# Attention, then routed experts on one core: another order of work where the two meet

## The chip, the cores and the metric

The kernel runs on one core of a Trainium2 chip. The metric is device microseconds (us) of one execution; the kernel before has a median of 485.14 us over three runs (483.79 to 489.23). TensorE does the matmuls, VectorE, ScalarE and GpSimd the elementwise work, and SP issues most of the transfers. In the profile they are PE (PEld for its weight loads), DVE, ACT, POOL and SP.

## The reference

Attention with sinks and a window, then a two-level choice of one expert out of 16 for each of the 3072 tokens:

```
q, k, v: 4 batches x 8 heads x 768 positions x 64
scores = q k^T / 8, kept where key is a sink (first 4) or 0 <= row - key < 128
a = softmax(scores);  attn = a v;  x = attn as 3072 tokens x 512
group = argmax(x w_group) of 4;  expert = argmax(x w_expert[group]) of 4
y = max(x w1[expert], 0) w2[expert]          w1: 512 x 1024, w2: 1024 x 512
out = softmax weight of the group * softmax weight of the expert * y
```

## The kernel before

Everything is one function, moe_attention, whose instructions are written in the order in which each engine is to run them (the class Pinned keeps it so). All its instructions are recorded at line 104, the wrapper; they are told apart by the tiles that they write and read.

**Attention** is a software pipeline over 24 tiles of 128 positions, with all eight heads of a tile together. The loop `for i in range(NI + 2)` works in step i on tile i (scores, maxima, exponentials), on tile a = i - 1 (transposes, values) and on tile b = i - 2 (normalising, routing logits). The helpers of a step are: `scores` (PE, tile ps), `maxima` (DVE, tile sm), `exps` (ACT, tile pt), `trans` (PE transposes of pt into tp), `evac` (ACT copy tp to pw), `halves` (POOL product of pw with a triangle), `sink_copy` (POOL), `sink_t` and `sink_evac` (PE and ACT, tile spT), `values` (PE, 32 small products pw with vv into po), `sink_values` (PE, 8 products into po), `out_evac` (ACT copy of po to xT), `natural` (PE transposes of xT into another part of po), `logits` (PE, xT with wsd), `norm` (DVE product of po with rc into xt, then a store by SP to xd in DRAM), `norm_logits` (DVE, tile lw) and `add_heads` (POOL additions into lt, DVE for the last tile).

**Routing** runs for six tiles at a time (`route_batch`). It is a generator of small DVE steps; `routing(k, kinds)` runs up to k of them and stops at one whose kind is not in kinds: "pe" are steps that need products (counts from oh, and the token table from af and bf), "rd" steps that read their results, "hv" the two heavy steps that build bf (DVE) and af (POOL). For the batch of tiles 12 to 17, those of the last steps before the experts, the POOL instructions are held in a list until the first "hv" step.

**Experts.** Weight chunks (128 rows of w1, 256 of w2) come by DMA into tiles rw. `wjob` splits one into a high part (whi, ACT cast) and the remainder (wlo, DVE subtraction). While attention runs, `wjob` converts half of a chunk and leaves the other half in the list `half`; from step NI = 24 on it converts a whole one. Three products (high by high, high by remainder, remainder by high) make one product of full precision. The first part of the first expert has 256 tokens. Its work is the generator `early_work`, called ew: the first `next(ew)` transposes the gathered rows xg (PE), the second splits them into un (ACT and DVE, with the gate cg), and every further one is one block of 12 matmuls of layer 1 (tile ph) with its activation (ACT) and, one block later, its split (DVE). There are eight blocks.

**The entry** is steps 24 and 25, in which no new tile is started. The attention's PSUM for scores is closed and a pool of four banks for ph is opened (`tail`). What is issued there on PE before: in step 24 transposes of xg, values of tile 22 (second half of the heads), sink and pt transposes of tile 23, natural and logits of tile 22, block 0, values and sinks of tile 23, block 1, block 2; in step 25 the six products of the token table, natural and logits of tile 23, blocks 3 and 4. The remaining blocks follow behind the loop.

A planner sets the rest of the order: `state["clk"]` counts what PE has been given, `state["dve"]` what DVE has; `spend` issues routing steps and conversions as long as DVE is no more than DVELAG = 1.5 us behind, and `prefetch` issues weight loads as raw tiles come free. A product that needs a chunk not yet converted forces its conversion (`weights`).

Of the kernel before, what the change touches and what calls it, by code (L numbers as in the profile page):

```python
# [24 lines left out]
NT = S // P  # L25
NI = B * NT
# [25 lines left out]
RAW, RAWB = 5, 6  # L52
# [2 lines left out]
DVELAG = 1.5  # L55
XLEAD = 9
PEGAP = 1.6
REND, TSTEP = 8, 16
HC = 3
LATE = 6  # L60
PELAG = 2.0
# [21 lines left out]
MAXB = 6  # L83
# [50 lines left out]
def moe_attention(tc, kqT, vN, vS, nsw, wgx, w1, w2, out):  # L134
    nc = Pinned(tc)
    v = nc.vector
    with ExitStack() as top, ExitStack() as att:
# [33 lines left out]
        vts, svs, env, bat = {}, {}, {}, {}  # L171
# [178 lines left out]
        gates = []  # L350
# [330 lines left out]
        def gather(r, j):  # L681
            w = min(P, CAPT[r] - j * P)
            cc = BASE[r] + j
            xg[r, j] = t = gp.tile([P, XW], F32, name="xg")
            src = xd[0:sum(BATCHES[:(SNAP if j < EC else SNAPB) + 1]) * P] if r == 0 else xd
            nc.gpsimd.indirect_dma_start(
                out=t[0:w], out_offset=None, in_=src,
                in_offset=bass.IndirectOffsetOnAxis(ap=gidx[0:w, cc:cc + 1], axis=0))
# [106 lines left out]
        def maxima(i, g, between=lambda k: None):  # L795
            t = i % NT
            e = env[i]
            if t:
                v.copy_predicated(psb[g][:, :, SW + NSK:3 * BW], selu[:, None, :].to_broadcast([P, 4, D]), psb[g][:, :, NSK:BW])
            between(0)  # L800
            e["sm", g] = sm = wk.tile([P, 4, SW], F32, name="sm", bufs=2)
            for k in range(4):
                h, s = head(g, k), k % 2 * NSK
                v.tensor_tensor_reduce(
                    sm[:, k], psb[g][:, k, BW + s:3 * BW + s], msk[:, min(t, 2), s:SW + s], -0.125, 3.0e38,
                    ALU.add, ALU.min, e["st"][:, h:h + 1])
                if k % 2:
                    between(k)
# [30 lines left out]
        def halves(i, g):  # L839
            pw = env[i]["pw", g]  # L840
            if i % NT:
                nc.gpsimd.tensor_tensor(pw.rearrange("p (k b) q -> p k b q", k=3)[:, ::-2],
                                        pw[:, None, 0:4].to_broadcast([P, 2, 4, D]),
                                        tri[:, :, None, :].to_broadcast([P, 2, 4, D]), ALU.mult)
# [30 lines left out]
        def values(i, g):  # L875
            pw = env[i]["pw", g]
            new, old = vts[i], vts.get(i - 1) if i % NT else None
            quarters(g, 0, P, new[:, 0], lambda d, j: pw[d, 2 * j:6 + 2 * j:5], start=g == 0)
            quarters(g, D, D, new[:, 1], lambda d, j: pw[d, 1 + 2 * j], stop=g == 1 and old is None)
            if old is not None:  # L880
                quarters(g, 0, P, old[:, 1], lambda d, j: pw[d, 4 + 2 * j:10 + 2 * j:5])
                quarters(g, 0, D, old[:, 0], lambda d, j: pw[d, 8 + 2 * j], stop=g == 1)
# [58 lines left out]
        def routing(k, kinds=(None, "pe", "rd", "hv")):  # L941
            while k > 0:
                if not rb or not have.issuperset(rb[0][0]):
                    return False
                kind = rb[0][2] if isinstance(rb[0][2], str) else None
                if kind not in kinds or (kind == "pe" and state["clk"] < state["at"]):
                    return False
                rb[0][2] = r = next(rb[0][1], "end")
                k -= r if isinstance(r, int) else 1
                if tail:  # L950
                    dve(0.6 if kind == "rd" else 0.25)
                state["at"] = max(state["clk"] + state["gap"], state["dve"] + 0.4)
                if rb[0][2] == "end":
                    rb.pop(0)
            return True
# [280 lines left out]
        def unit(k):  # L1236
            if quota[0] > 0 and routing(1, (None,)):
                quota[0] -= 1
# [11 lines left out]
        for i in range(NI + 2):  # L1250
            live = i < NI
            state["step"] = i
            quota[0] = REND
            a, b = i - 1, i - 2
            mid, old = 0 <= a < NI, 0 <= b < NI
            state["clk"] += 3.0
            if i == NI:
                flush()
                state.update(gap=0.0, dve=state["clk"])
                sps.close()  # L1260
                put_gates(MAXB)
                while later:
                    gather(*later.pop(0))
                ps_h = fl.enter_context(tc.tile_pool(name="ps_h", bufs=4, space=PSUM, side="right", reuse_waits="tile"))
                tail.append(ps_h)
            if live:
                scores(i, 0)
            if mid:
                evac(a, 0)
            if i == NI:  # L1270
                next(ew)
            if old:
                if b < NI - 1:
                    values(b, 1)
                out_evac(b)
            if i == NI:
                routing(TSTEP // 2, (None,))
                next(ew)
                if half:
                    half.pop()()()  # L1280
            if live:
                load_v(i)
                scores(i, 1)
                issue()
                maxima(i, 0, lambda k: unit(k) if k and i % NT == 3 else None)
                warm(FILL[i] if i < len(FILL) else 0, tp2[:, 0, 256:448])
            if mid:
                sink_copy(a)
                halves(a, 0)
            if i == NI + 1:  # L1290
                state["at"] = 0.0
                routing(1, ("pe",))
            if mid:
                sink_t(a)
                trans(a, 1)
            if live:
                exps(i, 0, (0, 1))
            if mid:
                evac(a, 1)
                sink_evac(a)  # L1300
            if live:
                exps(i, 0, (2, 3))
            if mid and not live:
                halves(a, 1)
            if not live and later and not gates:
                gather(*later.pop(0))
            late = None
            if live:
                late = half.pop()() if half else wjob()
                if half and i % NT == 0:  # L1310
                    first, more = late, half.pop()
                    late = lambda: (first(), more()())
            if i == 0:
                late_consts()
            if i == 1:
                routing_consts()
            if live:
                maxima(i, 1, lambda k: unit(k) if k == 1 or k and i % NT != 3 else None)
            if old:
                natural(b)  # L1320
            state["clk"] += 3.0
            if old:
                logits(b)
            if live and mid:
                values(a, 0)
            if i % 2 == 0 and 0 < i <= NI:
                sums(i - 1)
            if not live:
                norm(b)
                norm_logits(b)  # L1330
                next(ew)
            if mid and not live:
                values(a, 0)
            add_heads()
            routing(1, ("pe",))
            if mid:
                sink_values(a)
            if live and old:
                norm_logits(b)
            if live:  # L1340
                if mid:
                    halves(a, 1)
                flush()
                exps(i, 1)
                trans(i, 0)
                fill((2, 1, 4)[i % 2 * 2 if i % NT != 2 else 1] if i < NI - 1 else 0)
                if old:
                    norm(b)
                if later and not gates:
                    gather(*later.pop(0))  # L1350
                put_gates(2)
                got = bool(rb) and rb[0][2] == "rd" and routing(1, ("rd",))
                if late:
                    late()
                elif not (got and "tab" in state["read"]):
                    fill(2 if i % 2 else 3)
            else:
                if mid:
                    values(a, 1)
                    next(ew)  # L1360
                put_gates(MAXB)
                routing(TSTEP // 2 if mid else TSTEP, (None, "rd", "hv"))
            if old:
                del env[b]
            if i >= CHOOK:
                prefetch(min(RAW, len(raws) + (1 if live else RAW)))
            if not live:
                wjob()
                next(ew, None)
# [295 lines left out]
```

## Time and profile before

| | |
|---|---|
| median of three runs | 485.14 us |
| profiled execution | 485.14 us |
| span from its first to its last instruction | 483.3 us |
| PE busy | 464.7 us (96%) |
| DVE, ACT, POOL busy | 340.3, 325.9, 164.4 us |
| mean granted TensorE clock | 0.993 |

The profiled execution's time is the whole of the execution, the span what the trace covers. A granted clock of 1.00 is 2.4 GHz, 0.50 is 1.2 GHz. PE's busy time comes from modelled ends of pipelined matmuls, so that a slow clock shows as busy and not as idle time. Times in the rows are from the span's start.

### The profile page before, as it was taken

How to read it: one execution, taken by the hardware profiler on the slowest of the kernel's cores; microseconds unless marked ns; L12 is line 12 of the kernel's file. 1: busy time of each engine (PE TensorE's matmuls, PEld its weight loads, DVE VectorE, ACT ScalarE, POOL GpSimd, SP SyncE). 2: the span in 40 equal slices, each digit the busy share in tenths (PEclk: the TensorE clock that was granted, in tenths of full speed). 3: DMA queues.
4: the chain of work that ended last, by engine and by line, in shares of the span. 5: the costliest groups of instructions: out<-in, count | busy, mean ns of one | idle time of the engine just before them, and what ended most of it. 6: DMA issues, size and time to landing. Idle time of an engine off the chain costs nothing.

```text
span 483.3 us, 15521 instructions
## 1 busy us (share of the span) xinstructions
PE 464.7 (96%) x5865; PEld 396.4 (82%) x5865; DVE 340.3 (70%) x1144; ACT 325.9 (67%) x875; POOL 164.4 (34%) x269
## 2 busy tenths in 40 slices
PE   7999999999899999999999999999999999999994
PEld 6887788877778988989888778797979788977893
DVE  6766886887987799882274166564798887787960
ACT  4898889889892454762374176556788777687951
POOL 3463684674655023232303034102302260106021
PEclk9999999999998999999999999999999999999998
DMA  6566566677863379793224378859959997777100
GB/s 194 172 208 199 187 203 194 212 238 235 296 219 88 126 242 356 256 395 139 71 84 130 144 238 318 301 197 336 389 181 400 412 386 248 275 226 282 62 25 31
DMA packets 49556, 107.47 MB, mean 222 GB/s; under 512 B 8932, under 2 KB 9444, under 8 KB 49472
## 3 DMA queue, kind: packets, MB, share of 16 engines
q1 hardware_dynamic: 45008, 93.17, 56.1%
q0 software_dynamic: 4320, 12.94, 7.4%
q8 instruction: 48, 0.79, 0.7%
q14 instruction: 36, 0.29, 0.2%
q10 hardware_dynamic: 144, 0.28, 0.2%
HBM read 93.58 MB, written 12.93 MB: 220 GB/s over the span
## 4 chain that ended last, share of the span: by engine, by line
PE 74%; DVE 8%; issue 8%; ACT 7%; POOL 1%; DMA 1%; POOLq 0%; SPq 0%; DVEq 0%; ACTq 0%
PE po L104 32%; PE ph L104 30%; PE tp L104 6%; PE ps L104 6%; ACT pt L104 3%; DVE sm L104 2%; ACT whi L104 1%; DVE wlo L104 1%; DVE ps L104 1%; DVE xt L104 1%; POOL out L104 1%; ACT xT L104 1%; ACT pw L104 1%; DVE un L104 1%; DMA kb<-in_kqT 1%
## 5 line engine op out<-in xcount | busy, mean ns | idle before, releaser
L104 DVE TENSOR_TENSOR wlo<-rw,whi 128x1024 fp32r<-128x1024 f32 (+1 forms) x116 | 135.3, 1189 | 29.4 <-ACT whi L104 28.8
L104 PE MATMUL ph<-un,whi 128*128 128x256 f32 (+9 forms) x576 | 129.9, 315 | 1.2 <-DVE cg L104 1.2
L104 PE MATMUL po<-whi,un 128*128 128x512 f32 (+6 forms) x384 | 126.3, 394 | 0.0
L104 ACT CAST whi<-rw 128x1024 fp32r<-128x1024 f32 (+1 forms) x116 | 114.8, 1018 | 7.5 <-PE po L104 4.4
L104 POOL DMA_INDIRECT out<-ot,sidx x33 | 40.8, 1236 | 220.3 <-ACT ot L104 163.5
L104 PE MATMUL ph<-un,wlo 128*128 128x160 f32 (+10 forms) x416 | 100.2, 266 | 0.0
L104 PEld LDWEIGHTS ph<-un,whi 128*128 128x128 f32 x576 | 94.9, 191 | 3.6 <-DVE cg L104 1.4
L104 PEld LDWEIGHTS po<-whi,un 128*128 128x128 f32 (+5 forms) x384 | 69.8, 183 | 19.4 <-issue 2.1
L104 ACT ACTIVATE pt<-sm,st 128x136 f32<-128x136 f32 x192 | 76.3, 404 | 5.7 <-DVE st L104 5.5
L104 PE MATMUL po<-wlo,un 128*128 128x512 f32 (+7 forms) x200 | 77.8, 389 | 0.0
L104 PEld LDWEIGHTS ph<-un,wlo 128*128 128x128 f32 x416 | 77.4, 191 | 0.5
L104 POOL TENSOR_TENSOR pw<-pw,tri 128x512 f32<-128x512 f32 x40 | 51.2, 1281 | 12.1 <-ACT pw L104 11.3
L104 DVE CUSTOM_DVE_ANT_0 sm<-ps,msk 128x136 f32<-128x136 f32 x192 | 46.7, 295 | 6.9 <-ACT xT L104 1.3
L104 POOL DMA_INDIRECT xg<-xd,gidx x33 | 36.4, 1103 | 31.0 <-DMA rw<-in_w 15.8
L104 PE MATMUL po<-pw,vv 64*64 64x128 f32 (+1 forms) x1408 | 41.2, 251 | 2.5 <-DVE xt L104 1.7
L104 PEld LDWEIGHTS po<-pw,vv 64*64 64x64 f32 x1408 | 35.3, 134 | 9.0 <-issue 4.5
L104 PE MATMUL ps<-kb,qb 64*64 64x204 f32 (+1 forms) x768 | 41.5, 331 | 0.9 <-DVE lw L104 0.7
L104 PEld LDWEIGHTS po<-wlo,un 128*128 128x128 f32 (+6 forms) x200 | 35.8, 179 | 7.8
L104 ACT ACTIVATE un<-ph 128x256 fp32r<-128x256 f32 (+1 forms) x40 | 15.3, 382 | 38.8 <-PE ph L104 38.5
L104 DVE TENSOR_TENSOR hc<-ph,hc 128x160 f32<-128x160 f32 (+6 forms) x64 | 21.6, 338 | 25.8 <-ACT hc L104 25.8
L104 ACT ACTIVATION_READ_ACCUMULATOR pt<-sm,st 128x1 f32 x192 | 37.1, 193 | 0.0
L104 ACT ACTIVATE ot<-po,cg 128x512 f32<-128x512 f32 (+7 forms) x25 | 17.0, 679 | 25.8 <-PE po L104 25.7
(226 smaller groups left out, 655.1 us busy)
## 6 DMA issues: line engine op xcount, KB each, us to landing
rw<-in_w SPq DMA_DIRECT2D x128, 512.0 KB, 5.8
kb<-in_kqT SPq DMA_DIRECT2D x23, 272.0 KB, 3.7
qb<-in_kqT SPq DMA_DIRECT2D x24, 256.0 KB, 3.8
vv<-in_vN SPq DMA_DIRECT2D x24, 256.0 KB, 3.5
xd<-xt SPq DMA_DIRECT2D x24, 256.0 KB, 2.6
xg<-xd,gidx POOLq DMA_INDIRECT x33, 6.0
out<-ot,sidx POOLq DMA_INDIRECT x33, 5.8
sv<-in_vS SPq DMA_DIRECT2D x4, 128.0 KB, 4.9
```

What stands on the lines that cost most here:

```text
L104: r = f(*a, **k)
```

## The change

Three edits. In the attention a conversion is always one half per step: the branch that ran both halves in a step on a batch's first tile is gone. With it, routing steps between the maxima of a tile's second head group are left out behind the last maximum on the third tile of a batch too. At the entry, step 24 becomes a block of its own: values, sinks and values of tile 23 are issued ahead of block 0, chunk 3 is converted as a whole ahead of them if it hasn't been, four routing steps run early (EARLY) and twelve at the end, and the block ends with blocks 0 and 1. Step 25 keeps its order, with two blocks. The diff, without lines that only go because step 24 has its own block:

```diff
-REND, TSTEP = 8, 16
+REND, TSTEP, EARLY = 8, 16, 4
...
                 tail.append(ps_h)
+                evac(a, 0)
+                next(ew)
+                values(b, 1)
+                out_evac(b)
+                sink_copy(a)
+                halves(a, 0)
+                sink_t(a)
+                trans(a, 1)
+                evac(a, 1)
+                sink_evac(a)
+                halves(a, 1)
+                routing(EARLY, (None,))
+                sums(a)
+                natural(b)
+                logits(b)
+                norm(b)
+                state["clk"] += 3.0
+                next(ew)
+                if half:
+                    half.pop()()()
+                while state["done"] < 4:
+                    wjob(True)
+                values(a, 0)
+                add_heads()
+                norm_logits(b)
+                sink_values(a)
+                values(a, 1)
+                next(ew)
+                put_gates(MAXB)
+                routing(TSTEP - EARLY, (None, "rd", "hv"))
+                del env[b]
+                prefetch(RAW)
+                wjob()
+                next(ew)
+                continue
...
-            if i == NI:
-                routing(TSTEP // 2, (None,))
-                next(ew)
-                if half:
-                    half.pop()()()
...
                 late = half.pop()() if half else wjob()
-                if half and i % NT == 0:
-                    first, more = late, half.pop()
-                    late = lambda: (first(), more()())
...
-                maxima(i, 1, lambda k: unit(k) if k == 1 or k and i % NT != 3 else None)
+                maxima(i, 1, lambda k: unit(k) if k == 1 or k and i % NT not in (2, 3) else None)
...
             if not live:
                 norm(b)
                 norm_logits(b)
                 next(ew)
-            if mid and not live:
-                values(a, 0)
...
             else:
-                if mid:
-                    values(a, 1)
-                    next(ew)
                 put_gates(MAXB)
-                routing(TSTEP // 2 if mid else TSTEP, (None, "rd", "hv"))
+                routing(TSTEP, (None, "rd", "hv"))
```

## Rows read from the trace of the kernel before

**Rows 1.** Stretch, length, busy PE, PEld, DVE, ACT, POOL; granted clock, DMA share, GB/s.

```profile
129.00:130.00 1.00, 0.33 (x16) 0.34 (x17) 1.00 (x2) 0.41 (x1) 1.00 (x1) 1.00 1.00 367
...
145.80:147.00 1.20, 1.20 (x5) 1.20 (x6) 1.20 (x2) 0.00 (x0) 1.20 (x2) 0.50 0.00 0
146.00:156.00 10.00, 9.66 (x137) 8.98 (x137) 6.43 (x16) 2.56 (x5) 5.34 (x12) 0.84 0.31 86
```

**Rows 2.** TensorE's instructions at the entry: start us, us, form, idle before and its releaser.

```profile
145.79 0.58 PE L104 MATMUL ph<-un,whi 128*128 128x256 f32 x1 [1.24 <-DVE cg L104]
...
148.44 1.23 PE L104 MATMUL po<-pw,vv 64*64 64x128 f32 x32
...
151.08 0.50 PE L104 MATMUL ph<-un,whi 128*128 128x256 f32 x2
...
154.06 0.77 PE L104 MATMUL ph<-af,bf 128*128 128x112 f32 x6
155.17 0.46 PE L104 MATMUL po<-ident,xT 64*128 64x64 f32 x8 [0.34 <-ACT xT L104]
...
156.16 0.51 PE L104 MATMUL ph<-un,whi 128*128 128x256 f32 x2
```

**Rows 3.** the order of time in steps 18 and 19, all engines.

```profile
110.99 0.61 ACT L104 CAST whi<-rw 128x512 fp32r<-128x512 f32 x1
...
111.50 0.58 ACT L104 COPY pw<-tp 128x512 f32<-128x512 f32 x1
111.64 0.69 DVE L104 TENSOR_TENSOR wlo<-rw,whi 128x512 fp32r<-128x512 f32 x1 [0.84 <-ACT whi L104]
...
111.98 0.59 ACT L104 COPY xT<-po 128x512 f32<-128x512 f32 x1
...
113.04 0.41 ACT L104 ACTIVATE pt<-sm,st 128x136 f32<-128x136 f32 x1 [0.48 <-DVE st L104]
```

**Rows 4.** ScalarE's copies to xT in steps 12, 13 and 18.

```profile
71.89 0.59 ACT L104 COPY xT<-po 128x512 f32<-128x512 f32 x1 [0.56 <-PE po L104]
...
77.85 0.58 ACT L104 COPY xT<-po 128x512 f32<-128x512 f32 x1 [0.30 <-PE po L104]
...
106.21 0.59 ACT L104 COPY xT<-po 128x512 f32<-128x512 f32 x1 [0.86 <-PE po L104]
```

**Rows 5.** the order of time at the entry around the token table, all engines.

```profile
148.96 0.42 DVE L104 SCALAR_TENSOR_TENSOR un<-ph,un 128x256 fp32r<-128x256 f32 x1 [0.57 <-ACT un L104]
...
150.29 1.11 DVE L104 TENSOR_TENSOR bf<-colm,row 128x384 fp32r<-128x384 f32 x2
...
150.94 1.85 POOL L104 TENSOR_TENSOR af<-oh,av 128x336 fp32r<-128x336 bf16 x2
...
152.82 0.38 ACT L104 ACTIVATE un<-ph 128x256 fp32r<-128x256 f32 x1 [3.89 <-PE ph L104]
...
153.10 1.04 ACT L104 CAST whi<-rw 128x1024 fp32r<-128x1024 f32 x1
```

**Rows 6.** the order of time, VectorE beside GpSimd at the entry.

```profile
145.18 1.27 POOL L104 TENSOR_TENSOR pw<-pw,tri 128x512 f32<-128x512 f32 x1 [1.81 <-ACT pw L104]
...
145.72 1.28 DVE L104 TENSOR_TENSOR wlo<-rw,whi 128x512 fp32r<-128x512 f32 x1
...
146.41 1.15 POOL L104 TENSOR_TENSOR lw<-lw 128x80 f32<-128x80 f32 x2
...
152.75 0.71 POOL L104 TENSOR_TENSOR lw<-lw 128x80 f32<-128x80 f32 x2
```

**Rows 7.** the order of time to the second expert's first product, TensorE and VectorE.

```profile
168.56 0.61 PE L104 MATMUL ph<-whi,un 128*128 128x512 f32 x2
...
169.24 0.61 PE L104 MATMUL ph<-whi,un 128*128 128x512 f32 x2
...
189.01 1.22 DVE L104 TENSOR_TENSOR wlo<-rw,whi 128x1024 fp32r<-128x1024 f32 x1
...
190.28 0.38 PE L104 MATMUL ph<-un,wlo 128*128 128x248 f32 x1
```

More of the change, by code (lines that the diff above doesn't have):

```diff
@@ L1269, in moe_attention @@
                 evac(a, 0)
-            if i == NI:
-                next(ew)
             if old:
-                if b < NI - 1:
+                if live:
                     values(b, 1)
                 out_evac(b)
-            if i == NI:
-                routing(TSTEP // 2, (None,))
-                next(ew)
-                if half:
-                    half.pop()()()
             if live:
@@ L1289, in moe_attention @@
                 halves(a, 0)
-            if i == NI + 1:
+            if not live:
                 state["at"] = 0.0
@@ L1302, in moe_attention @@
                 exps(i, 0, (2, 3))
-            if mid and not live:
-                halves(a, 1)
-            if not live and later and not gates:
-                gather(*later.pop(0))
             late = None
@@ L1325, in moe_attention @@
                 values(a, 0)
-            if i % 2 == 0 and 0 < i <= NI:
+            if i % 2 == 0 and 0 < i < NI:
                 sums(i - 1)
@@ L1331, in moe_attention @@
                 next(ew)
-            if mid and not live:
-                values(a, 0)
             add_heads()
@@ L1357, in moe_attention @@
             else:
-                if mid:
-                    values(a, 1)
-                    next(ew)
                 put_gates(MAXB)
-                routing(TSTEP // 2 if mid else TSTEP, (None, "rd", "hv"))
+                routing(TSTEP, (None, "rd", "hv"))
             if old:
```

## The prediction

> **What bounds the kernel now.** I read the stretches by stage first. TensorE is busy for 464.7 of 483.3 us, and in the page's forty slices it shows 9 tenths or more nearly throughout, so a microsecond won at the experts' entry (139 to 156 us) travels to the end unless a later wait takes it back. At the entry itself TensorE looks busy too, but its clock is at 0.50 of full speed, the 1.2 GHz level, from 145.8 us on, and the mean over 146 to 156 us is 0.84 [rows 1]. What the low level costs is (1 - 0.84) x 10 us plus half of the 0.2 us before 146: 1.7 us.
>
> The order of time shows why. TensorE has done the first of the twelve matmuls of the first expert block (call the blocks f0 to f7) when it idles 1.24 us, until the second half of the gathered rows is split on VectorE; the clock falls at that moment. f0's other eleven matmuls then take 148.44 - 145.79 = 2.65 us, the 72 small attention products 2.64 us, f1 and f2 together 154.06 - 151.08 = 2.98 us, so 1.49 us for a block at 2.4 GHz. A later wait of 0.34 us, for the transposed tile 23, stands ahead of f3, which starts at 156.16 us [rows 2]. Recoverable at the entry: 1.24 + 0.34 + 1.7 = 3.3 us. That is all the reorder can aim at, 0.7% of the time.
>
> **Part 1: halves.** Before, step 18 converted both halves of weight chunk 0, every later step one half. Now each step converts one, so chunk 3 reaches the entry untouched. What goes at step 18: one cast, after which ScalarE's next copy starts 111.50 - 110.99 = 0.51 us later, and on VectorE a subtraction with an idle 0.84 us before it. Without the cast the next copies start at 110.99 and 111.47 us, the second ends 0.59 us later, at 112.06, and the exponentials of step 19 could start there instead of at 113.04: 0.98 us. VectorE's part isn't what holds them then: it comes free earlier by its idle time and its subtraction, 0.84 + 0.69 = 1.53 us [rows 3]. Upper bound 1.5. Lower bound 0: step 18 with its two casts lasts 111.98 - 106.21 = 5.77 us from one copy of xT to the next, the same kind of step without any cast (step 12) 77.85 - 71.89 = 5.96 [rows 3, 4]. I take 1.0, because the chain of rows at 111 to 113 us is direct, while step 12 has waits of its own. The routing step shifted behind the maxima of step 20 is the same VectorE work a little later: nothing, inside these bounds.
>
> The price comes at the entry: chunk 3 as one conversion of 1024 columns (1.04 us on ScalarE [rows 5]) instead of a half. On TensorE it costs nothing, since values and sinks run meanwhile; its VectorE time is in part 2.
>
> **Part 2: the order at the entry.** Removed: f0 no longer waits, as the 72 small products stand ahead of it. At 2.4 GHz they take 2.64 - 0.42 = 2.2 us (f0 lost 2.65 - 11/12 x 1.49 = 1.28 of the 1.7, they the rest). TensorE was free at 144.55; the norm of tile 22 now stands ahead of the first values, and these write the bank that it reads. I allow 0.35 us for that (the copy-to-transpose wait of 0.34 is the nearest row [rows 2]; bounds 0 and the 0.69 of a norm-sized subtraction [rows 3]). Then 144.55 + 0.35 + 2.2 + 1.4 (rest of f0) + 1.5 (f1) = 150.0: TensorE is at the end of f1, where before it began f1 at 151.08.
>
> Added: directly behind f1 now stand the six list products (ph from af and bf, the token table of tiles 12 to 17), ahead of the natural transposes and of f2. Before, f2 lay in front of them. When is af there? VectorE starts bf at 150.29 before. Out of its queue fall the 0.57 us wait and 0.42 us of f0's split (now behind bf) [rows 5], and the 0.6 us by which the half subtraction was held up (1.28 against 0.69 [rows 6, 3]); in come 0.53 for the whole chunk (1.22 against 0.69 [rows 7, 3]). So bf starts 1.06 us sooner, near 149.3 (rounded to the late side), and as af ends 150.94 + 1.85 - 150.29 = 2.5 us after bf's start [rows 5], af is complete at 151.8 at best.
>
> It will be later, because chunk 4's subtraction stands on VectorE right behind bf and reads two SBUF operands while GpSimd works on af. What such a pair does is in the trace: the subtraction at 145.72 started on VectorE while GpSimd ran a multiplication until 146.45, took 1.28 instead of 0.69 us, and the next two GpSimd additions took 1.15 instead of 0.71 [rows 6]. The waiting VectorE instruction got its turn between two of GpSimd's. Its cast is ready (f0's activation at 148.5, plus 0.38 and 1.04 [rows 5]: 150.0). So the second af waits 1.22 us more, until 153.0. Behind it on TensorE's queue wait the transposes, the logits of tile 23 and f2. TensorE idles from 150.0 to 153.0 but for 0.35 us of the first three products. Then 0.3 for the last three, 156.16 - 155.17 = 1.0 for transposes and logits, 1.5 for f2: f3 starts at 155.8, against 156.16. At a held clock all the reordering is worth 0.36 us: the stall has moved from f0 to the lists.
>
> And the clock? Rows show it falling after idle pieces of 1.24 us and less, and holding in a microsecond of attention in which TensorE was busy for 0.33 [rows 1, 2]. The new stall idles longer than the old, so I expect the low level again. Bounds 0 and 1.7; I take 1.0, as part of a low stretch would fall on the stall itself. Entry: -0.36 + 1.0 = +0.6.
>
> The Trainium skill (TensorE: Matmul & The Clock Gate, "HAM oscillation — how this bites in real kernels") lays the low level to a single idle gap longer than any in this stretch, before or after. By that rule the clock would now hold, which is rival (b), and the sum would be 484.1; but by it the clock would not have fallen before either, and the trace shows that it did.
>
> **What else moves.** On SP's queue tile 22's store goes ahead of chunk 8's load; that load waits for chunk 3's conversion, at 145.72 + 1.28 = 147.0 before [rows 6] and, by the sums above, about as late after. GpSimd's second multiplication of tile 23 goes ahead of where it stood; the gathers left over are issued at the entry's head as before. One block fewer is issued inside the two steps, and by the planner's own bookkeeping, followed by hand from the entry to the end of f7, VectorE stands further behind than before (18.0 against a clock of 14.8, before 15.7 against 13.4; chunk 3's 1.2 us is most of it), so its rule (VectorE at most 1.5 us behind) lets the last count product go one inner step of the next part later: three products, 0.7 us [rows 7]. VectorE's last routing chain follows that product and ends with chunk 11 at 189.01 + 1.22 = 190.23, and the first product that needs it starts at 190.28 [rows 7]: no slack. Cost 0 to 0.7; I take 0.3.
>
> **Sum.** The profiled execution has 485.14 us (span 483.3, 1.84 around it), which is also the median of the runs. 485.14 - 1.0 + 0.6 + 0.3 = 485.0: no change. A change below 1% of the time (4.85 us) can't be told from none here; the runs before spread from 483.79 to 489.23.
>
> **Rivals.** (a) af gets through first and the clock holds: f3 starts 1.2 us sooner, at 154.6, so -1.56 at the entry: 485.14 - 1.0 - 1.56 + 0.3 = 482.9. For it: GpSimd has its next instruction queued; against: the order at 146.4. 17%. (b) The stall as forecast, but the clock holds: 485.14 - 1.0 - 0.36 + 0.3 = 484.1. For it: TensorE works without a break from the first values to f1's end, ahead of the stall; against: the fall after only 1.24 us. 20%. (c) Slower: at 190 us the second expert's first product waits for its weights. The planner, believing VectorE busier, puts two conversions more (2 x 1.22) behind the routing chain; without slack there TensorE waits for all of it: 485.0 + 2.4 = 487.4. It decides from the point at which chunk 11 ends after 190.2 less TensorE's own lead. Against it: need forces a conversion early in the program. 10%. (d) The halves do nothing, since step 18 is no longer than step 12: 486.0. 15%. That the reorder isn't what the queues do is excluded: each engine keeps program order.
>
> **Numbers.** Forecast 35%, the rest (3%) unknown. The range reaches from 482.5, below (a), to 487.0, above (d) with the clock's full 1.7; (c) stays out. Faster by over 1% would need more than all 3.3 us plus all of part 1: 5%. Slower by over 1% is (c) with every bound at its worst: 6%. Within 1%: 89%.
>
> **What will show it.** Right: in the changed profile f0's block starts with no wait and runs at 2.4 GHz; TensorE then idles 2 to 3 us ahead of the list products, the releaser being GpSimd's af, with a VectorE subtraction of chunk 4 between the two afs; step 18 shows one cast and its exponentials start 1 us sooner. Wrong: no such idle time (then a), or a fall of the clock already ahead of f0, or waits on weight splits near 190 us (then c).

## The result: 0.6% slower, where no change was forecast

| | before | after |
|---|---|---|
| median of 20 runs each | 486.21 us | 488.98 us |
| lowest to highest | 483.75 to 489.23 | 486.79 to 491.16 |
| profiled execution | 485.14 us | 490.31 us |
| its span | 483.3 us | 488.5 us |
| its mean granted TensorE clock | 0.993 | 0.992 |

The ratio is 1.0059, with a 95% interval from 1.0039 to 1.0079: slower, by less than the 1% that the chances took for their bound, but outside the range that was forecast (482.5 to 487.0). The two profiled executions lie 5.2 us apart, the medians 2.8: the profile of before is a run of the faster half, that of after one of the slower. So the traces tell where time went, and the sizes are settled by the medians of the experiments. Three executions in the sets of the experiments, of 733, 877 and 1112 us, are slow runs and are left out of the medians and ratios below.

Two landmarks cut each trace into three parts: ScalarE's copy to xT in step 24, which ends the attention steps, and the first product of the first expert's second layer.

| profile | copy to xT, step 24 | from there to the second layer | from there to the end of the span |
|---|---|---|---|
| before | 142.54 | 27.4 | 313.4 |
| after | 143.00 | 30.0 | 315.5 |

So the steps cost 0.5 us more, the entry 2.6, and what follows 2.1. The stretches of the kernel after, first those that answer to [rows 1], then those in which the clock was low (columns as there):

```profile
145.80:147.00 1.20, 1.20 (x36) 1.01 (x32) 1.20 (x3) 0.36 (x1) 0.50 (x2) 1.00 0.70 244
146.00:156.00 10.00, 7.74 (x106) 6.86 (x95) 7.57 (x19) 2.34 (x5) 4.96 (x10) 0.87 0.44 121
...
152.00:153.00 1.00, 0.30 (x3) 0.16 (x2) 1.00 (x2) 0.00 (x0) 1.00 (x1) 1.00 0.22 19
153.00:154.00 1.00, 0.53 (x3) 0.53 (x3) 0.12 (x1) 0.00 (x0) 0.92 (x3) 0.67 0.20 19
154.00:156.00 2.00, 2.00 (x27) 1.70 (x26) 0.69 (x1) 0.00 (x0) 0.30 (x2) 0.50 0.62 173
156.00:158.00 2.00, 2.00 (x9) 2.00 (x10) 1.75 (x9) 0.00 (x0) 0.00 (x0) 0.50 0.59 225
158.00:160.00 2.00, 2.00 (x12) 2.00 (x11) 1.80 (x8) 1.11 (x2) 1.01 (x1) 0.50 0.08 21
160.00:161.00 1.00, 1.00 (x10) 1.00 (x10) 0.76 (x1) 0.26 (x2) 0.00 (x0) 0.92 0.80 237
```

The clock that stood at 0.50 from 145.8 us on before is full there now. It falls some 7 us later, while TensorE idles ahead of the second three list products, and stays low longer: the cost is 0.33 + 3 x 2 x 0.50 + 0.08 = 3.4 us, twice the 1.7 of before. Next the order of time of the same run (TensorE, VectorE and GpSimd; start us, us, idle before and its releaser); it answers to [rows 2, 5, 7]:

```profile
147.53 0.51 PE L104 MATMUL ph<-un,whi 128*128 128x256 f32 x2
...
149.94 1.10 DVE L104 TENSOR_TENSOR bf<-colm,row 128x384 fp32r<-128x384 f32 x2
150.59 2.82 POOL L104 TENSOR_TENSOR af<-oh,av 128x336 fp32r<-128x336 bf16 x2
150.97 1.82 DVE L104 TENSOR_TENSOR wlo<-rw,whi 128x1024 fp32r<-128x1024 f32 x1
151.76 0.54 PE L104 MATMUL ph<-af,bf 128*128 128x112 f32 x3 [1.08 <-POOL af L104]
153.47 0.89 PE L104 MATMUL ph<-af,bf 128*128 128x112 f32 x3 [1.17 <-POOL af L104]
154.29 0.69 PE L104 MATMUL po<-ident,xT 64*128 64x64 f32 x8
...
174.29 1.22 DVE L104 TENSOR_TENSOR wlo<-rw,whi 128x1024 fp32r<-128x1024 f32 x1
...
180.28 1.22 DVE L104 TENSOR_TENSOR wlo<-rw,whi 128x1024 fp32r<-128x1024 f32 x1
181.55 0.50 PE L104 MATMUL po<-wlo,un 128*128 128x512 f32 x1 [2.48 <-DVE wlo L104]
...
196.53 0.38 PE L104 MATMUL ph<-un,wlo 128*128 128x248 f32 x1 [0.34 <-DVE wlo L104]
```

f0 starts without a wait. Between the two af stands chunk 4's subtraction, and TensorE waits once for each af. The new thing is at 181.55 us: a product of the first expert's second layer waits 2.48 us for the subtraction of chunk 7, which began at 180.28. In the kernel before, chunks 6 and 7 stood on VectorE right behind each other (its order of time):

```profile
170.14 0.50 DVE L104 TENSOR_TENSOR af<-oh,av 128x336 fp32r<-128x336 bf16 x1
170.56 2.35 DVE L104 TENSOR_TENSOR wlo<-rw,whi 128x1024 fp32r<-128x1024 f32 x2
```

After, the routing chain has got between them.

### The profile page after: what moved, and what is told of

Read it like the earlier page. It is cut to its first block, busy times and chain, and to the rows that moved or that the text cites. A ratio compares the mean times of both kernels' runs of the same rounds, so it can differ in the third digit from the quotient of the medians.

```text
span 488.5 us, 15518 instructions
## 1 busy us (share of the span) xinstructions
PE 467.1 (96%) x5865; PEld 398.0 (81%) x5865; DVE 341.3 (70%) x1143; ACT 325.9 (67%) x874; POOL 164.0 (34%) x269
## 4 chain that ended last, share of the span: by engine, by line
PE 68%; DVE 13%; issue 8%; ACT 6%; DMA 2%; POOL 2%; POOLq 0%; SPq 0%; DVEq 0%; ACTq 0%
PE po L104 29%; PE ph L104 28%; PE ps L104 6%; PE tp L104 5%; DVE wlo L104 3%; ACT pt L104 3%; DVE sm L104 2%; ACT whi L104 1%; DVE xt L104 1%; DVE un L104 1%; DMA rw<-in_w 1%; POOL out L104 1%; DMA ni<-in_nsw 1%; ACT pw L104 1%; DVE ps L104 1%
## 5 line engine op out<-in xcount | busy, mean ns | idle before, releaser
L104 ACT ACTIVATE ot<-po,cg 128x512 f32<-128x512 f32 (+7 forms) x25 | 17.0, 680 | 29.8 <-PE po L104 29.7
```

The source lines that it names most:

```text
L104: r = f(*a, **k)
```

## The experiments

Theory T has two places: the wait for the lists with the clock's fall behind it, and chunk 7, which the planner moves because chunk 3, now converted whole at the entry, is booked as 1.2 us of VectorE's time. The medians of before in the three sets of runs were 485.36, 485.06 and 485.53 us.

| run | ratio to before, 95% | copy to xT, step 24 | to the second layer | to the end |
|---|---|---|---|---|
| halves_only | 1.0019 (0.9988 to 1.0050) | 141.56 | 26.7 | 313.3 |
| order_only | 1.0011 (0.9989 to 1.0034) | 143.53 | 28.1 | 313.1 |
| after_uncounted | 1.0020 (1.0001 to 1.0040) | 142.66 | 28.5 | 313.4 |
| lists_later | 1.0037 (1.0013 to 1.0061) | 142.75 | 25.9 | 317.2 |
| lists_later_uncounted | 0.9938 (0.9916 to 0.9959) | 142.58 | 25.8 | 312.7 |
| after_filled | 1.0059 (1.0035 to 1.0083) | 141.31 | 27.1 | 318.1 |
| after_filled_uncounted | 0.9962 (0.9937 to 0.9987) | 144.46 | 27.3 | 313.7 |
| af_alone | 1.0063 (1.0042 to 1.0083) | 141.03 | 27.7 | 315.7 |
| order_lists_later | 0.9965 (0.9947 to 0.9983) | 144.15 | 25.8 | 312.7 |
| halves_only_uncounted | 1.0014 (0.9986 to 1.0042) | 140.58 | 27.8 | 312.0 |
| halves_again | one run, 490.0 us | 144.45 | 29.8 | 314.0 |
| fill_shift | one run, 490.06 us | 142.05 | 29.7 | 316.6 |

**Each half of the change alone.** `halves_only` is the kernel before with the first edit, chunk 3 whole at its entry; `order_only` the kernel after with the old halves.

```diff
 halves_only, against before
-                if half and i % NT == 0:
-                    first, more = late, half.pop()
-                    late = lambda: (first(), more()())
...
+                while state["done"] < 4:
+                    wjob(True)
...
-                maxima(i, 1, lambda k: unit(k) if k == 1 or k and i % NT != 3 else None)
+                maxima(i, 1, lambda k: unit(k) if k == 1 or k and i % NT not in (2, 3) else None)
```

```diff
 order_only, against after
+                if half and i % NT == 0:
+                    first, more = late, half.pop()
+                    late = lambda: (first(), more()())
...
-                maxima(i, 1, lambda k: unit(k) if k == 1 or k and i % NT not in (2, 3) else None)
+                maxima(i, 1, lambda k: unit(k) if k == 1 or k and i % NT != 3 else None)
```

> The kernel before with the first edit alone: always one half per step (and the routing step left out on the third tile), chunk 3 converted whole at the entry, ahead of the first block; the order of the entry as before. Differences to before in us. Theory T (the change loses in two places, the list products at the entry with the clock, 2 to 3 us, and chunk 7's conversion put behind the last routing chain, 2.5 us, and wins 1.0 us by the halves): -1.0, between -1.5 and -0.3; step 18 to 20 shorter by 1 us. Rival H (the halves win nothing): 0 to +0.6, the whole chunk 3 showing at the entry.

> The kernel after, with both halves in the first tile's step and the old routing steps put back: only the entry's order is changed, and chunk 3 comes to it half converted. Chunk 7 then stands where it stood before. T: +2.5 against before (+1.5 to +3.5): TensorE waits some 2.5 us for the list products and the clock falls. Rival P (all the loss is chunk 7's place): 0 to +0.5. Rival E (all the loss is the entry, the halves' win included): +3.9.

Neither came out as T had it: the halves won nothing in the median (1.0019, which Rival H allows), and the order lost 0.5 us and not 2.5. Chunk 7 is in time in `order_only` (313.1), since without the whole chunk 3 nothing is booked, and in its profile the low clock cost less: the mean is 0.92 in 150 to 156 and in 156 to 172 us, 0.08 x 22 = 1.8 us.

**Chunk 7 in time.** One line behind the forced conversion:

```diff
+                state["dve"] -= 1.2
```

> The kernel after, with one line: chunk 3's conversion at the entry is not added to the planner's VectorE clock (1.2 us less). Chunk 7 is then issued directly behind chunk 6, as before the change. T: against before +0.4 (-0.5 to +1.3), that is 2.5 below the kernel after; no wait of TensorE on a weight's remainder near 181 us; the wait for the list products stays. P: -1.0 to 0. E: +2.9, as the kernel after.

1.0020 against 1.0059 for the kernel after: 1.9 us, and the last part of the trace is 313.4 again. That the booking moved chunk 7, and that it costs about 2 us, is shown. The waits for the lists are as in the kernel after (VectorE and TensorE in order of time, then stretches):

```profile
151.41 0.54 PE L104 MATMUL ph<-af,bf 128*128 128x112 f32 x3 [1.10 <-POOL af L104]
153.13 0.54 PE L104 MATMUL ph<-af,bf 128*128 128x112 f32 x3 [1.17 <-POOL af L104]
...
171.18 2.35 DVE L104 TENSOR_TENSOR wlo<-rw,whi 128x1024 fp32r<-128x1024 f32 x2
```

```profile
153.00:154.00 1.00, 0.87 (x12) 0.74 (x12) 0.00 (x0) 0.00 (x0) 0.84 (x4) 0.97 0.17 17
154.00:156.00 2.00, 2.00 (x24) 1.92 (x21) 1.50 (x4) 0.00 (x0) 0.04 (x1) 0.50 0.83 238
156.00:158.00 2.00, 2.00 (x14) 2.00 (x13) 1.79 (x11) 0.22 (x1) 0.74 (x1) 0.66 0.44 164
```

The low clock behind the same two waits cost 0.03 + 2 x 0.50 + 2 x 0.34 = 1.7 us here, where it cost 3.4 in the profile of the kernel after.

**The lists behind f2.** The routing step that issues the six list products is taken out of the place between f1 and the transposes:

```diff
                 state["at"] = 0.0
-                routing(1, ("pe",))
```

> The kernel after, with the list products issued behind block f2 instead of ahead of the transposes of tile 23. T: the wait of 2.3 us for af becomes one of some 1 us for the copy of tile 23, the low clock at most one stretch as before the change; the wait of 2.5 us for chunk 7 stays: against before 0 (-1.0 to +1.5), some 3 below the kernel after. P: +2.9, since the entry is worth nothing. E: -1.5 to 0.

In the profiled run the entry is mended, and the clock falls at the next wait instead. Stretches of this run:

```profile
150.00:156.00 6.00, 5.05 (x59) 4.73 (x58) 5.54 (x16) 2.52 (x5) 4.13 (x7) 1.00 0.23 43
...
172.00:180.00 8.00, 5.52 (x22) 4.21 (x22) 7.38 (x29) 1.87 (x3) 2.23 (x3) 0.90 0.94 334
180.00:190.00 10.00, 10.00 (x45) 8.19 (x45) 6.46 (x22) 4.40 (x7) 1.79 (x2) 0.91 0.98 356
```

The part up to the second layer is 4.1 us shorter than in the kernel after, but the rest takes 317.2 us for 315.5: the same wait of 2.48 us for chunk 7 now has a low clock behind it, 0.10 x 8 + 0.09 x 10 = 1.7 us. Not every run did this. A fall that costs 1.7 us takes 1.7 / 485 = 0.0035 off the mean clock, and five of the twelve runs have a mean of 0.998 or 0.999; their median is 485.45 us, that of the seven others 487.58. In the median of all the gain over the kernel after is 1.1 us, where T had some 3.

**Both repairs**, the last two diffs together.

> Both repairs in one kernel: the list products behind the third inner step of the first expert's first layer, and chunk 3's conversion not counted, so that chunks 6 and 7 are converted one right behind the other. Theory T (two separate losses that add): each repair took its part alone (0.4% and 0.2%), so the ratio to the kernel before is 0.997 to 1.000, no clock drop at 153 to 160 us, no wait of chunk 7's product, and the profile's clock at 0.995 or above. Rival I (one loss, seen twice: whatever removes a wait of 2 us of TensorE has the whole effect): no better than the first repair alone, 1.002. Rival C (the clock falls somewhere else as soon as it holds at the entry): 1.002 to 1.004, with a fall of the clock in another stretch.

482.68 us, 0.6% faster than the kernel before. This is more than T's sum (alone the repairs took 0.39% and 0.22%, together 1.21%), below T's range, and the opposite of the rivals: the wait for chunk 7 is gone, one of 0.95 us for the transposed tile 23 is left at the entry, and the clock holds at both places. All 12 runs had a mean clock of 0.996 or more, where the kernel after had 0.988 to 0.995. That wait and two stretches of its trace:

```profile
151.19 0.46 PE L104 MATMUL po<-ident,xT 64*128 64x64 f32 x8 [0.95 <-ACT xT L104]
```

```profile
150.00:156.00 6.00, 5.05 (x59) 4.73 (x58) 5.50 (x17) 2.34 (x5) 3.80 (x6) 1.00 0.25 27
...
172.00:180.00 8.00, 8.00 (x36) 6.52 (x36) 7.28 (x32) 3.52 (x4) 2.98 (x3) 1.00 1.02 352
```

**The clock without the wait.** Ahead of the list products TensorE gets work that nobody reads:

```diff
                 state["at"] = 0.0
+                warm(24, tp2[:, 0, 256:448])
                 routing(1, ("pe",))
```

> The changed kernel with 24 products of zeros (bf16, about 0.08 us each, results not used) issued to TensorE ahead of the list products. They lie in the wait for the first af, so that TensorE has only the second wait of 1.17 us left; the data waits are unchanged. Theory T (the clock's fall is the larger part of the entry's loss): no fall of the clock at 153 to 160 us or one as short as in the kernel before, list products no earlier, ratio 1.001 to 1.003 with chunk 7 still late. Rival S (the stall itself is the loss): the list products end where they did, clock or no clock, and the ratio stays at 1.005 to 1.007.

TensorE's order of time at the entry, and its stretches:

```profile
148.83 2.15 PE L104 MATMUL tp<-wz 128*128 128x192 bf16 x24
150.77 0.52 PE L104 MATMUL ph<-af,bf 128*128 128x112 f32 x3
151.80 0.54 PE L104 MATMUL ph<-af,bf 128*128 128x112 f32 x3 [0.51 <-POOL af L104]
```

```profile
150.00:156.00 6.00, 5.49 (x65) 5.18 (x64) 4.43 (x15) 1.01 (x2) 3.04 (x6) 1.00 0.33 52
...
172.00:180.00 8.00, 5.52 (x21) 4.16 (x21) 7.38 (x29) 1.69 (x3) 2.21 (x3) 0.88 1.02 353
180.00:190.00 10.00, 10.00 (x46) 8.14 (x46) 6.21 (x22) 4.54 (x7) 1.77 (x2) 0.93 0.94 348
```

One wait of 0.51 us is left, and the second three products end where they did, counted from the copy to xT. The clock held at the entry, 2.8 us of the 30.0 are gone there, and some 2.5 of them came back behind chunk 7, where it fell (318.1 us for 315.5). The ratio stayed at 1.0059, as the rival had it, but in the profiled run not for its reason. Four of the twelve runs have a mean clock of 0.998, so that in them it fell at neither place. The run that separates them has `state["dve"] -= 1.2` as well, and chunk 7 in time:

> The changed kernel with the 24 products of zeros ahead of the list products and with chunk 3 not counted, so that chunk 7 is in time; the list products stay where the change has them and wait as they did. Theory T (the fall of the clock is what two repairs share: with the entry filled it fell at chunk 7's wait instead, 0.88 and 0.93 in the two stretches behind it): with neither wait long the clock holds at both places, and only the wait for the list products is left, about 1 us more than with the lists moved: ratio 0.995 to 0.998. Rival S (the place of the list products is the loss, the clock a companion): 1.001 to 1.003, as with chunk 3 not counted alone.

0.9962, as T said: with the lists where the change put them, and with their data as late as before, the products of zeros and chunk 7's old place turn 1.0059 into a gain. Against `after_uncounted` the products of zeros alone are worth 1.0020 - 0.9962 = 0.58%, 2.8 us. The wait for the lists is the smaller part of the entry's loss (1.2 us, 0.9962 against 0.9938 with the lists moved, though these intervals overlap), the clock behind it the larger. That the 24 products also move everything behind them in TensorE's stream of instructions was not tested apart.

**The two af undisturbed.** The conversion of chunk 4 goes to the end of the step behind:

```diff
                 prefetch(RAW)
-                wjob()
                 next(ew)
                 continue
...
             if not live:
                 wjob()
+                wjob()
                 next(ew, None)
```

> The changed kernel with the conversion of chunk 4 at the end of the following step, so that VectorE has nothing to read while GpSimd makes the two af. Theory T: the two af then take about 1.85 us as in [rows 5] instead of 2.82, both triples of list products come as one block near 152.5, TensorE's idle time there falls from 2.3 to about 1.2 us, and the time by 1 us at full clock; if the clock still falls at about 153 us, only that. Chunk 7 is still late. Ratio to the kernel before 1.003 to 1.005 with the fall, 0.999 to 1.001 without. Rival N: the subtraction is not what splits the pair, the second af still ends near 153.4 and the ratio stays at 1.006.

In the trace it is as T had it (GpSimd, then TensorE):

```profile
148.63 1.84 POOL L104 TENSOR_TENSOR af<-oh,av 128x336 fp32r<-128x336 bf16 x2
...
149.80 0.54 PE L104 MATMUL ph<-af,bf 128*128 128x112 f32 x3 [1.09 <-POOL af L104]
150.53 0.54 PE L104 MATMUL ph<-af,bf 128*128 128x112 f32 x3 [0.20 <-POOL af L104]
```

The pair takes 1.84 us for 2.82, so it is the subtraction that splits it. But the clock fell all the same (stretches of this run):

```profile
150.00:156.00 6.00, 5.80 (x51) 5.50 (x51) 4.12 (x17) 1.04 (x2) 2.29 (x5) 0.72 0.21 53
152.00:153.00 1.00, 1.00 (x8) 1.00 (x5) 1.00 (x4) 0.00 (x0) 0.00 (x0) 0.51 0.06 4
```

It fell at 152.0 us, when TensorE had been at work again since 150.5, behind waits of 1.09 and 0.20 us. The median is no better than that of the kernel after. T's 1 us did not show; why the other runs give it back is open, since the profiled one was the fastest of the twelve.

**What the halves are worth.** The mended entry with the old halves, which is `order_only` without the `routing(1, ("pe",))` that `lists_later` leaves out:

> The both-repairs kernel's entry with the old placing of the conversions in the attention steps (halves of two chunks at one place in the fourth step, as before the change): it tells what of the win at 0.9938 comes from the halves and what from the order at the entry. Theory T: the steps lose 1.0 us again (0.2%), the entry's order keeps its part: ratio 0.995 to 0.997. Rival O (all of it is the order; halves give nothing that lasts, as the halves alone at 1.002 suggest): 0.993 to 0.995. Rival H (the order alone gives nothing, as the order alone at 1.001 suggests): 0.999 to 1.001.

0.9965 with the old halves, 0.9938 with the new: 1.3 us for the halves, where T had 1.0, though the intervals overlap. The order alone, mended, is worth 1.7 us.

The first edit alone with chunk 3 not counted (`state["dve"] -= 1.2` again):

> The first edit alone, with chunk 3's conversion at the entry not counted, so that every later chunk of the first expert comes one place earlier in VectorE's order. With it counted the second expert's first layer waited 0.83 us at 189.6 us for a subtraction. Theory T: that wait goes, 0.5 to 0.8 us: ratio 1.000 (0.998 to 1.002). Rival F (the first edit's win is lost because the clock falls a second time in half of the runs: 0.988 to 0.992 there against 0.996 to 0.999): the two groups remain and the ratio too, 1.001 to 1.003.

The wait near 190 us is gone (312.0), but the rival was right about the time: 1.0014, eleven of the twelve runs at clocks from 0.986 to 0.996, the twelfth at 0.940. Two groups, as the rival had them, do not show any more. So `halves_only` once more, unchanged, for a second profile:

> The first edit alone once more, for a second profile: its runs fell into two groups, about 484 us at a clock of 0.996 to 0.999 and about 488 us at 0.988 to 0.992, and the profile taken was of the first group (481.6 us of span). Theory T: if this one is of the second group, it shows two more falls of the clock, at the entry's first products (146 to 150 us) or at the wait of the second expert's first layer (190 us); if it is of the first group, none there. Rival R: the groups differ by pauses of TensorE and not by the clock, and the stretches show the same clock in both.

And a look at a pause that the trace gives no releaser for:

```diff
-FILL = [8, 10, 6]
+FILL = [16, 10, 6]
```

> The changed kernel with 8 more products of zeros at the first step (16 for 8), in a wait near the start; nothing else. It looks at the pause of 0.87 us, without any waiter or releaser, between the 20th and the 21st of the 32 products of the values in step 22. Theory F (the pause is at a fixed place of TensorE's stream of instructions): the pause, if there is one, comes after the 12th product. Rival D (it is at that product for a reason of its data): still after the 20th. Rival M (it is at a fixed time): at 133.1 to 133.5 us whatever the product. One run: no statement on time.

The second profile has 490.0 us at a clock of 0.988. Order of time of TensorE in step 22, then stretches of the same run:

```profile
131.16 0.77 PE L104 MATMUL po<-pw,vv 64*64 64x128 f32 x20
133.62 0.55 PE L104 MATMUL po<-pw,vv 64*64 64x128 f32 x12 [1.69 <-issue]
```

```profile
135.00:139.00 4.00, 4.00 (x74) 3.42 (x76) 2.93 (x13) 0.86 (x2) 1.78 (x3) 0.57 0.54 172
149.00:155.00 6.00, 5.05 (x72) 4.15 (x75) 4.39 (x13) 0.38 (x1) 4.39 (x9) 0.50 0.45 134
```

TensorE pauses in the middle of the 32 products of the values, the clock falls behind that, and again at the entry. In the first profile neither is there. Rival R's pauses and T's falls of the clock are both in the slower profile. With eight products of zeros more near the start, the pause stands eight products earlier (`fill_shift`, order of time of TensorE):

```profile
131.12 0.55 PE L104 MATMUL po<-pw,vv 64*64 64x128 f32 x12
132.41 0.67 PE L104 MATMUL po<-pw,vv 64*64 64x64 f32 x20 [0.75 <-issue]
```

So, by this one run, it belongs to a place in TensorE's stream of instructions and not to these data or to a time. T had named the entry and 190 us for the falls; step 22 it had not.

## Why the prediction was wrong

**Part 1, the halves: the size was right, its way to the end was not.** Step 18 has lost its second cast. ScalarE's copies to xT in the kernel after, and the first exponentials of step 19:

```profile
106.92 0.59 ACT L104 COPY xT<-po 128x512 f32<-128x512 f32 x1 [0.86 <-PE po L104]
...
112.16 0.59 ACT L104 COPY xT<-po 128x512 f32<-128x512 f32 x1
112.64 0.42 ACT L104 ACTIVATE pt<-sm,st 128x136 f32<-128x136 f32 x1
...
117.43 0.59 ACT L104 COPY xT<-po 128x512 f32<-128x512 f32 x1
```

The exponentials wait for nothing now and start 112.64 - 106.92 = 5.72 us behind the copy of step 18, for 113.04 - 106.21 = 6.83 before [rows 3, 4]: 1.1 us sooner, where the prediction had 0.98. From copy to copy it is 112.16 - 106.92 = 5.24 us for 5.77 [rows 3, 4]; the step behind it 5.27 for 5.90. Together 1.16 us; forecast 1.0. The run came 0.7 us late to step 18 (106.92 for 106.21; the trace of `order_lists_later`, with the old halves, is 1.1 us late there), and four steps later a pause like those above, 0.87 us here, takes most of the gain back; so xT of step 24 is no sooner. Rival (d), that the halves do nothing, fits the medians of the first edit alone, but not the trace; with the entry mended the medians give the halves 1.3 us.

**Part 2, order of the queues: right.** No wait ahead of f0, f0 and f1 at full clock, the subtraction between the two af, TensorE waiting for GpSimd: 1.08 + 1.17 = 2.25 us idle, forecast 2.65 (150.0 to 153.0 less 0.35). The Trainium skill (SBUF — State Buffer, "Who interferes with whom") says that a VectorE instruction with two SBUF inputs contends with a GpSimd instruction that reads SBUF, and that the shared ports are an exclusive lock; the trace agrees, with 1.82 us for a subtraction of 1.22 and 2.82 for a pair of 1.84.

**Part 2, the clock: the step that failed.** It was bounded by 1.7 us, the cost in the trace of before, and taken at 1.0. But that bound was the cost of one fall after one wait of 1.24 us, and nothing in the rows held it there. Measured: 3.4 us in the profile, 2.8 by the entry's part in the profiles of `after_filled` and the kernel after, and 2.8 in the medians with chunk 7 in time. The length of the waits does not explain it: behind the same two waits the low clock cost 3.4 us in the profiles of the kernel after and of `fill_shift` (1.09 and 1.18 us), and 1.7 in that of `after_uncounted`. One event gave no bound on the cost. The rule of the Trainium skill (TensorE: Matmul & The Clock Gate, "HAM oscillation — how this bites in real kernels"), by which gaps as short as these leave the clock alone, did not hold here either: no idle piece ahead of the fall is longer than 1.17 us.

**What else moves, the second step that failed: rival (c)'s mechanism, one expert earlier.** The prediction followed the planner's bookkeeping, found VectorE 3.2 us behind its clock with most of the rise from chunk 3, and drew only the last count product from it (0.3 us). The same rule holds back conversions. It held back one, chunk 7, for 2.1 us; (c) had two, at 190 us, for 2.4 and 10%. At its own place there is 0.34 us (196.53). That need forces a conversion early in the program was the argument against (c). In the code (`weights`) need forces it only where its product is issued, and in the trace routing steps fill VectorE from 176.8 to 180.3 us, right up to chunk 7's subtraction. The term was 0.3 us, for the last count product; chunk 7 alone cost about 2.

**The sum.** In the profile: steps +0.5 (forecast -1.0), entry +2.6 (+0.6), the rest +2.1 (+0.3). The forecast named both mechanisms, and its range held neither the clock's 3.4 us nor a wait like (c)'s. It also added the costs, and the medians do not add: the repairs gave 0.39% and 0.22% alone and 1.21% together. In two profiles the clock that held at the entry fell at chunk 7 instead.

## What to carry to other kernels

When a wait of TensorE goes and another comes, price the clock behind the new one by an experiment over several executions, and don't cap it by what an old one cost in one trace; where two such waits stand one behind the other (28 us apart here), mend both before judging either. Where a planner works from bookkeeping, a changed entry in it is a change of its own: follow it to every item that the same rule moves. An edit that seems to have no effect in the median may have won and lost: here two groups of runs at two clocks said so.

## What was not expected of the hardware

**The same waits cost one execution more than another.** Five profiles have the wait of 2.48 us for chunk 7 and differ at the entry. Where the clock had fallen at the entry (the kernel after, `af_alone`, `fill_shift`) it stayed at 1.00 behind chunk 7; where it had held (`lists_later`, `after_filled`) it fell there, to means of 0.90 and 0.91 and of 0.88 and 0.93. That is no rule: five of the twelve runs of `lists_later` and four of `after_filled` have a mean clock of 0.998 or more, so that it fell at neither place. And at the entry the same pair of waits cost 3.4 us in two profiles and 1.7 in a third. What decides is not shown.

**A pause of TensorE at a place of the program.** Ten of the fourteen profiles have it, of 0.18 to 1.69 us, two of them only as a longer group of products (for these the length is not given). The clock fell behind the two longest, 1.42 and 1.69 us, and held behind the others. In these ten the packet of the instruction queue q8 nearest ahead of it lies between 129.75 and 132.25 us, and TensorE goes on some 2.5 to 4 us behind it; in the four without a pause it lies between 128.5 and 129.5 us. The DMA share in 129 to 134 us is 0.75 to 1.02 in all fourteen, so it does not tell the ten from the four. That the instructions came late fits the packets' times; no run moved that packet, so it is argued and not shown.
